# Block products for two more experts in the last batch, joined score bursts, a backlog rule and more H buffers in an attention and expert-mixture kernel

## The chip, the cores and the metric

The kernel runs on one core of one Trainium2 chip. The metric is the device time of one execution in microseconds. Times are medians of several executions. The record calls an execution slow when it takes over 1.5% more than the fastest one of the same kernel.

A profile shows one execution. Its span is about 1.7 us shorter than the time of that execution, some 0.5 to 2.7 us shorter than the median of the kernel, and its first 35 us vary by up to about 2 us from execution to execution, with the moment at which the first loads arrive. For differences of one or two microseconds I therefore also use the part of each trace that begins with a fixed instruction, a score burst at about 35 us, up to which all kernels here have the same TensorE instructions (298 records in a trace, or 299 where one more 512-column record was kept).

## The reference

```python
def _attn_ref(q, k, v, n_sink, window):          # (4, 8, 768, 64), n_sink 4, window 128
    scores = q @ k.T / sqrt(D)
    keep = (pos_k < n_sink) | ((rel >= 0) & (rel < window))
    a = softmax(where(keep, scores, -1e9))
    return a @ v

def _moe_ref(x, domain_probs, w1, w2):           # x (3072, 512), 4 experts, F 1024
    p = domain_probs / (domain_probs.sum(-1, keepdims=True) + 1e-9)
    for e in range(4):
        h = np.maximum(x @ w1[e], 0.0)
        out += p[:, e:e+1] * (h @ w2[e])
```

The attention output, with its heads side by side, is the input `x` of the mixture. Every token goes through all four experts.

## The kernel before

A scheduler written in Python orders the instructions when the kernel is built. It keeps a planned clock for each engine, and at each step it picks the next piece of TensorE work. The four batches go through in turn; while the mixture of one batch runs, the attention of the next batch is mixed in. From batch 1 on, tokens come in groups of 256 (three groups a batch).

A *first-layer unit* is one expert's `relu(x @ w1)` for one group. A plain unit takes 32 matmuls of 256 columns. A *fast* unit is a scheme of seven block products (P1 to P7) where a plain one has eight: 56 matmuls of 128 columns, with sums of weights and of tokens formed by VectorE, and with more VectorE and ScalarE work on the results. `START` says from which batch an expert is fast. The second layer uses such a scheme for every expert from batch 1 on; these are *the products* below (112 matmuls of 256 columns for a group).

```python
START = {0: 1, 1: 2}
CHAIN = ("P1", "P2", "P6", "P5", "P7", "P4", "P3")
NH = 6                                    # H buffers (outputs of first-layer units)

def emit_fast(self, u, m, ready):         # cut: one block product of a fast unit
    name = {"P1": "X", "P5": "V", "P6": "X", "P2": "Y", "P7": "X", "P3": "V", "P4": "X"}[m]
    ...
    if m == "P1":   ...   # ScalarE seeds tile Y with a copy of P1
    elif m == "P5": ...   # ScalarE keeps P5
    # both():  VectorE tensor_add(V, c5, X); only then may P7 and P3 start
    elif m == "P7": ...   # VectorE tensor_add(c5, c5, y); only then may P4 start
    # four results: VectorE max(.,0) * gate

def emit_product(self):                   # cut: second-layer products, two accumulators
    bank = int(m in ("P2", "P5", "P3"))
    ...
        if m == "P1": nc.scalar.copy(out=acc[1][:, 0:G], in_=x)
        if m == "P3": nc.vector.tensor_add(C12, C12, x)          # then store
        nc.scalar.copy(out={"P2": C11, "P6": C12, "P7": C22, "P4": C21}[m], in_=x)
        # P7: then VectorE adds P5 from acc[1] to C22

# the main loop: options are (ready, rank, kind, step); the lowest rank that is ready goes first
opts = [(max(r, now), 0 if due else 3, "att", step) for r, step in att.options()]
opts.append((max(p, now), 1 if mix.credit >= QF * G else 2.5, "product", None))
opts += [(max(f, now), 2, "first", x) for f, x in mix.firsts()]
```

Scores of two heads (one *burst*) use TensorE in halves of 64 rows, sink scores in quarters of 32 columns; everything else uses the whole array.

In this kernel a *bank* is a buffer that a group of matmuls writes. Another engine must copy or add its content out (the *evacuation*) before another group may use it. Names in the profile lines: `hps` is the bank of a plain unit, `cps` of a block product, `acc` of the second layer, `sps` of scores, `sinks` of sink scores, `od` of attention outputs. `H` is a unit's result, `T` a sum of tokens, `S` a sum of parts of `H`, `osb` the finished output, `qkT` the transposed rows.

The softmax here doesn't subtract the row's maximum and nothing guards it: scores larger than these inputs give would overflow.

Of the kernel before, what the change touches and what calls it, by code (L numbers as in the profile page):

```python
# [16 lines left out]
def kernel(  # L17
# [43 lines left out]
    START = {0: 1, 1: 2}  # L61
    ONACT = 1
    BIASED = 1
# [237 lines left out]
    def weight_form1(e):  # L301
# [3 lines left out]
        if e not in forms1:  # L305
            x = wpool.tile([P, 3, NDB // 2, F // 2], BF16, name=f"vf_{e}", tag=f"vf_{e}")
            forms1[e] = {"P1": A11, "P2": A12, "P3": x[:, 2], "P4": A22, "P5": x[:, 0], "P6": x[:, 1], "P7": A21}
            formed1[e] = 0
# [15 lines left out]
    def form1_due(e):  # L324
        n = formed1.get(e, 0)
        return landed.get(("w1", e), 1e12) < t["pe"] and (n < 3 or n == 3 and not left1[e])
# [233 lines left out]
    def sinks(b, piece):  # L560
# [3 lines left out]
        q0, q1 = piece * G, (piece + 1) * G  # L564
        ready = max([free_at(), keys_at[b]] + turned(b, piece))
# [10 lines left out]
        def run(engine):  # L576
# [5 lines left out]
            sinkA_at[b, piece] = at  # L582
        later("act", done, 800, run)

    def scores(b, hp, g):
        T = qkT[b]
        w = sum(x[2] for x in GROUPS[g]) * P
        ready = scores_ready(b, hp, g)
# [22 lines left out]
        scored_at[b] = done = pe(w, ready, n=6, switch=2)  # L611
# [32 lines left out]
    def scores_ready(b, hp, g):  # L644
        return max(free_at(2), *turned(b, g, hp))
# [98 lines left out]
    class Attention:  # L744


        def __init__(self, b):
# [3 lines left out]
            for g in range(NG):  # L751
# [3 lines left out]
                if g:  # L755
                    self.todo.insert(2 - NHP if b == 0 else -NHP, ("sinks", b, g, 0))
# [3 lines left out]
        def more(self):  # L760
            return bool(self.todo or self.scored or self.valued)

# [5 lines left out]
        def options(self):  # L768
# [5 lines left out]
            if self.todo:  # L774
                kind, b, x, y = self.todo[0]
                if kind == "scores":
                    if len(self.scored) < 4:
                        yield scores_ready(b, x, y), "todo"
                elif kind == "keys":
                    yield max(turned(b, 0)), "todo"  # L780
                elif kind == "sinks":
                    yield max([free_at(), keys_at.get(b, 1e12)] + turned(b, x)), "todo"
# [3 lines left out]
        def emit(self, step):  # L786
# [10 lines left out]
            elif step == "flip":  # L797
                _, b, g, hp = self.flips.pop(0)
                transposes(b, g, hp)
                if (b, g, hp) == (1, NG - 1, 0):  # L800
                    nat_loads(2, range(NQB))
                    turns.extend((2, tb) for tb in range(NQB))
            else:
# [4 lines left out]
                elif kind == "sinks":  # L808
                    sinks(b, x)
# [23 lines left out]
    CHAIN = ("P1", "P2", "P6", "P5", "P7", "P4", "P3")  # L833
# [3 lines left out]
    class Mixture:  # L837


        def __init__(self):  # L840
# [19 lines left out]
            self.stored = []  # L860

# [5 lines left out]

        def early_ready(self, g):
            if not self.early[g] or self.live >= NH:
# [5 lines left out]
        def opened(self, b, g, e):  # L875

            self.H[b, g, e] = mo.tile([P, 2, QF, 2, P], BF16, name="H", tag="H", bufs=NH)
            self.live += 1
# [12 lines left out]
        def begin(self):  # L891
# [3 lines left out]
            if self.units and self.live < NH:  # L895
                self.open.append(self.opened(*self.units.pop(0)))

        def widen(self):

            u = self.open[0]  # L900
            if len(self.open) == 1 and u["unit"][0] and len(u["left"]) < len(UNITS) and self.units and self.live < NH:
# [195 lines left out]
        def chore(self):  # L1097
# [12 lines left out]
            if self.last:  # L1110
                b, g, e = u = self.last[0]
                if (b, g, "P5") not in self.products:
# [56 lines left out]
        def emit_product(self):  # L1169
# [13 lines left out]
            self.piece = (k + 1) % E  # L1183
            if k < E - 1:
                return
            self.products.pop(0)
            if m == "P1":
                out_sb[b, g] = mo.tile([P, 2, Dout], FP32, name="osb", tag="osb", bufs=1)
                r = (b * NQB + 2 * g) * P
                self.C22[b, g] = join(2, lambda at: nc.sync.dma_start(out=out[r + P:r + 2 * P, :], in_=out_sb[b, g][:, 1]))  # L1190
            o = out_sb[b, g]
            C11, C12, C21, C22 = o[:, 0, 0:G], o[:, 0, G:], o[:, 1, 0:G], o[:, 1, G:]
            if m == "P5":
                acc_free[1] = end
                return
# [4 lines left out]
            def run(engine):  # L1200
                if m == "P1":
                    nc.scalar.copy(out=acc[1][:, 0:G], in_=x)  # L1202
                    acc_free[0] = acc_free[1] = act(G, seeded)
                    return
                if m == "P3":
# [4 lines left out]
                    return  # L1210
                nc.scalar.copy(out={"P2": C11, "P6": C12, "P7": C22, "P4": C21}[m], in_=x)  # L1211
                acc_free[bank] = at = act(G)
                if m == "P4":
                    sp(at)
                    self.C22[b, g](at)
                if m == "P7":
                    def add(engine):
                        nc.vector.tensor_add(C22, C22, acc[1][:, 0:G])
                        acc_free[1] = dve(G)
                        self.C22[b, g](acc_free[1])  # L1220
# [184 lines left out]
```

## Time and profile before

| | before |
|---|---|
| median of 4 runs | 379.08 us (378.89 to 379.22) |
| profiled span | 376.6 us |
| TensorE busy | 98% |
| VectorE busy | 72% |

The page of the kernel before gives the busy time of each engine, and the head of its chain of waits (shares of the span by engine):

```profile
PE 367.4 (98%) x3947; PEld 298.6 (79%) x3959; DVE 269.5 (72%) x610; ACT 148.4 (39%) x386; POOL 71.4 (19%) x91
...
PE 81%; DMA 13%; POOL 4%; issue 1%; DVE 0%; ACT 0%; POOLq 0%
```

The Trainium skill, "Perfetto Trace Analysis", section "Identifying the Most-Contended Engine", warns that the busy share of matmuls is a bad measure of distance from the limit, because pipelined instructions look smaller in the trace. So 98% alone proves nothing. Two other views do. The table of waits shows what TensorE waited for (engine, result and line, releaser: us in total, times, longest):

```profile
PE acc L484 <- DVE lent L398: 1.4, 1, 1.4
PE sps L604 <- DVE qkT L222: 1.1, 1, 1.1
...
PE acc L1178 <- ACT osb L1211: 0.5, 1, 0.5
PE acc L1178 <- ACT acc L1202: 0.4, 1, 0.4
```

The first two lie in the first 10 us, the last two in the final run of products; the three left out are a wait of 0.9 us for a weight load at 18 us and two of 0.2 us, at 36 and 72 us. And the timeline (start, length, instructions; the length includes the modelled end of the last matmul, so the pace is read from start to start) shows the pace:

```profile
33.53 1.89 PE L1248 MATMUL acc<-w,H 128*128 128x512 bf16 x8
35.35 0.62 PE L604 MATMUL sps<-qkT 64*128 64x128 bf16 x12
35.90 0.29 PE L569 MATMUL sinks<-qkT,ksd 128*32 128x256 bf16 x4
...
246.44 0.61 PE L1038 MATMUL cps<-T,w 128*128 128x128 bf16 x8
246.98 0.39 PE L604 MATMUL sps<-qkT 64*128 64x128 bf16 x6
247.31 1.05 PE L961 MATMUL hps<-xT,w 128*128 128x256 bf16 x8
...
264.73 1.91 PE L1178 MATMUL acc<-w,S 128*128 128x256 bf16 x16
266.48 1.91 PE L1178 MATMUL acc<-wf,H 128*128 128x256 bf16 x16
...
276.99 0.61 PE L1038 MATMUL cps<-xT,w 128*128 128x128 bf16 x8
277.43 0.61 PE L1038 MATMUL cps<-T,vf 128*128 128x128 bf16 x8
```

Sixteen matmuls of 256 columns take 1.75 us (109 ns each), eight of 128 columns 0.45 us (56 ns each): both stream at nearly the same pace per column. A score burst does not: the one at 246.98 us comes 0.09 us after the eight matmuls ahead of it are through (246.44 + 0.45), and the next instruction 0.33 us after its start.

For the last batch, windows give each engine's busy time in a stretch, with the number of instructions in brackets:

```profile
core 0: us, PE busy (x) PEld busy (x) DVE busy (x) ACT busy (x) POOL busy (x), PEclk, DMA share, GB/s
250.00:350.00 100.00, 100.00 (x1147) 92.25 (x1148) 76.12 (x162) 18.84 (x46) 0.00 (x0) 1.00 0.14 40
300.00:310.00 10.00, 10.00 (x125) 9.33 (x124) 9.69 (x19) 1.07 (x2) 0.00 (x0) 1.00 0.17 56
310.00:320.00 10.00, 10.00 (x107) 9.11 (x105) 7.04 (x19) 2.18 (x5) 0.00 (x0) 1.00 0.09 27
320.00:330.00 10.00, 10.00 (x113) 9.19 (x112) 7.44 (x16) 1.82 (x4) 0.00 (x0) 1.00 0.24 68
330.00:340.00 10.00, 10.00 (x129) 9.38 (x128) 9.79 (x20) 1.43 (x3) 0.00 (x0) 1.00 0.09 28
340.00:350.00 10.00, 10.00 (x103) 9.06 (x102) 3.86 (x9) 1.49 (x4) 0.00 (x0) 1.00 0.05 18
```

VectorE is 76% busy on the mean but uneven: nearly full while first-layer units run, lighter while products do. TensorE does not stop in these 100 us all the same.

### The profile page before, as it was taken

How to read it: one execution, taken by the hardware profiler on the slowest of the kernel's cores; microseconds unless marked ns; L12 is line 12 of the kernel's file. 1: busy time of each engine (PE TensorE's matmuls, PEld its weight loads, DVE VectorE, ACT ScalarE, POOL GpSimd, SP SyncE). 2: the span in 40 equal slices, each digit the busy share in tenths (PEclk: the TensorE clock that was granted, in tenths of full speed). 3: DMA queues.
4: the chain of work that ended last, by engine and by line, in shares of the span. 5: the costliest groups of instructions: out<-in, count | busy, mean ns of one | idle time of the engine just before them, and what ended most of it. 6: DMA issues, size and time to landing. Idle time of an engine off the chain costs nothing.

```text
span 376.6 us, 9443 instructions
## 1 busy us (share of the span) xinstructions
PE 367.4 (98%) x3947; PEld 298.6 (79%) x3959; DVE 269.5 (72%) x610; ACT 148.4 (39%) x386; POOL 71.4 (19%) x91
## 2 busy tenths in 40 slices
PE   7899999999999999999999999999999999999995
PEld 3585767667666788888888888889999999999984
DVE  5664988666345997696599499579499496795780
ACT  4854633675655144436315545362112011111110
POOL 8935114743322093010010000000000000000000
PEclk9999999999999999999999999999999999999999
DMA  9999999959697999148295211122011110200101
GB/s 167 167 185 202 210 210 174 152 40 178 60 125 150 179 145 146 67 47 58 66 153 136 52 63 30 30 82 61 28 58 30 57 31 29 71 30 2 57 1 57
DMA packets 110807, 35.61 MB, mean 95 GB/s; under 512 B 94260, under 2 KB 106132, under 8 KB 110764
## 3 DMA queue, kind: packets, MB, share of 16 engines
q0 software_dynamic: 77520, 17.31, 50.9%
q1 hardware_dynamic: 32188, 17.18, 20.7%
q10 hardware_dynamic: 1056, 0.52, 0.5%
q8 instruction: 31, 0.51, 0.5%
q14 instruction: 12, 0.10, 0.1%
HBM read 40.45 MB, written 6.34 MB: 124 GB/s over the span
## 4 chain that ended last, share of the span: by engine, by line
PE 81%; DMA 13%; POOL 4%; issue 1%; DVE 0%; ACT 0%; POOLq 0%
PE acc L1178 30%; PE hps L961 25%; PE cps L1038 13%; DMA w<-in_moe_w_dram 12%; PE acc L1248 6%; PE sps L604 3%; PE od L670 2%; DMA qkn<-in_q_dram 1%; POOL qkn L186 1%; PE tr L502 1%; POOL w L264 1%; POOL vx L251 1%; PE od L663 1%; POOL w L274 0%; POOL sel L417 0%
## 5 line engine op out<-in xcount | busy, mean ns | idle before, releaser
L961 PE MATMUL hps<-xT,w 128*128 128x256 bf16 x1056 | 131.6, 273 | 1.0 <-DMA w<-in_moe_w_dram 0.9
L961 PEld LDWEIGHTS <-w 128*128 128x128 bf16 x1056 | 99.1, 98 | 15.7 <-issue 1.9
L1178 PEld LDWEIGHTS <-H 128*128 128x128 bf16 x720 | 67.8, 98 | 10.5 <-issue 3.0
L629 ACT ACTIVATE aT<-sps 128x512 bf16<-128x512 f32 (+1 forms) x96 | 48.3, 568 | 38.1 <-PE sps L604 38.0
L985 DVE SCALAR_TENSOR_TENSOR H<-hps,gates 128x512 bf16<-128x512 f32 x84 | 56.9, 684 | 2.4 <-PE hps L961 1.3
L1178 PE MATMUL acc<-w,H 128*128 128x256 bf16 x432 | 56.4, 273 | 0.4 <-ACT acc L1202 0.4
L709 ACT ACTIVATE onat<-od,R 128x64 bf16<-128x64 f32 x144 | 33.0, 324 | 36.1 <-DVE R L697 36.0
L1248 PE MATMUL acc<-w,H 128*128 128x512 bf16 x180 | 43.6, 379 | 0.7 <-issue 0.2
L1211 ACT COPY osb<-acc 128x256 f32<-128x256 f32 x36 | 13.5, 374 | 57.4 <-PE acc L1178 54.2
L1178 PE MATMUL acc<-wf,H 128*128 128x256 bf16 x288 | 35.2, 273 | 0.5 <-ACT osb L1211 0.5
L251 POOL DMA_DIRECT2D vx<-in_v_dram x24 | 21.3, 898 | 72.0 <-PE od L670 63.0
L623 DVE TENSOR_TENSOR aT<-aT,mask 128x1024 bf16<-128x1024 bf16 (+1 forms) x36 | 22.9, 640 | 16.4 <-ACT aT L629 16.4
L1248 PEld LDWEIGHTS <-H 128*128 128x128 bf16 x192 | 18.1, 98 | 17.8 <-issue 0.3
L1038 PEld LDWEIGHTS <-w 128*128 128x128 bf16 x480 | 30.8, 98 | 1.8 <-issue 0.6
L1057 DVE SCALAR_TENSOR_TENSOR H<-cps,gates 128x512 bf16<-128x512 f32 x45 | 30.7, 684 | 0.2
L1178 PEld LDWEIGHTS <-S 128*128 128x128 bf16 x288 | 27.6, 98 | 3.8 <-issue 0.5
L974 ACT ACTIVATE H<-hps 128x512 bf16<-128x512 f32 x35 | 20.9, 598 | 24.2 <-PE hps L961 23.8
L1066 ACT COPY cps<-cps 128x512 f32<-128x512 f32 x15 | 8.7, 581 | 45.1 <-PE cps L1038 45.1
L1260 DVE SCALAR_TENSOR_TENSOR osb<-acc,scale_t,osb 128x512 f32<-128x512 f32 x18 | 13.5, 750 | 17.7 <-PE acc L1248 16.1
L186 POOL DMA_DIRECT2D qkn<-in_q_dram x22 | 19.9, 904 | 20.4 <-PE tr L502 12.2
L1038 PEld LDWEIGHTS <-vf 128*128 128x128 bf16 x360 | 22.6, 98 | 0.6
L186 POOL DMA_DIRECT2D qkn<-in_k_dram x22 | 20.0, 908 | 8.7 <-DMA w<-in_moe_w_dram 8.5
(96 smaller groups left out, 435.2 us busy)
## 6 DMA issues: line engine op xcount, KB each, us to landing
w<-in_moe_w_dram POOLq DMA_DIRECT2D x7, 1024.0 KB, 18.9
out_dram<-osb SPq DMA_DIRECT2D x24, 256.0 KB
gates<-gate_rows SPq DMA_DIRECT2D x36, 128.0 KB
vx<-in_v_dram POOLq DMA_DIRECT2D x24, 128.0 KB, 6.5
qkn<-in_q_dram POOLq DMA_DIRECT2D x22, 128.0 KB, 6.3
qkn<-in_k_dram POOLq DMA_DIRECT2D x22, 128.0 KB, 6.2
w<-in_moe_w_dram POOLq DMA_DIRECT2D x2, 512.0 KB, 9.3
kraw<-in_k_dram ACTq DMA_DIRECT2D x2, 256.0 KB
```

The source lines that it names most:

```text
L186: nc.gpsimd.dma_start(out=both[:, i], in_=src[b, :, tb * P:(tb + 1) * P, :].rearrange("h p d -> p h d"),)
L251: nc.gpsimd.dma_start(out=vx[tb][:, :, 0:D], in_=v[b, :, tb * P:(tb + 1) * P, :].rearrange("h p d -> p h d"),)
L623: nc.vector.tensor_mul(a, a, m[:, None, :].to_broadcast([P, 2, w]))
L629: nc.scalar.activation(out=a[:, ph], in_=sps[ph][:, 0:w], func=AF.Exp, scale=scale)
L709: nc.scalar.mul(o[:, qi, hp, ph * D:(ph + 1) * D], od[:, qi, ph, 0:D], R[:, qi, ph])
L961: nc.tensor.matmul(h[:, i].rearrange("p (q n) -> p q n", q=2), lhsT=w1_sb[e][:, db, fb * P:(fb + 1) * P], rhs=xT[b, g][:, :, db], start=(i ...
L974: nc.scalar.activation(out=dst, in_=h, func=AF.Relu)
L985: nc.vector.scalar_tensor_tensor(out=dst, in0=h, scalar=0.0, in1=gate, op0=ALU.max, op1=ALU.mult,)
L1038: nc.tensor.matmul(y[:, f], lhsT=A[:, d, f * P:(f + 1) * P], rhs=T[:, d], start=(m in ("P1", "P5") and f == 0 and d == 0), stop=(d == 1), ...
L1057: nc.vector.scalar_tensor_tensor(out=dst, in0=src, scalar=0.0, in1=gate, op0=ALU.max, op1=ALU.mult)
L1178: nc.tensor.matmul(x, lhsT=self.operand(b, g, e, m)[:, f], rhs=forms[e][m][:, f], start=(k == 0 and f == 0 and m in ("P1", "P5")), stop=(k ...
L1248: nc.tensor.matmul(op, lhsT=H[:, fb // QF, fb % QF, s], rhs=w2_sb[e][:, fb, :], start=(fb == 0), stop=(fb == NFB - 1),)
```

## The change

The intent: less TensorE work (block products for experts 2 and 3 in the last batch; fewer changes of TensorE's tiling), and a schedule that can bear VectorE's larger share (products go ahead when VectorE is behind; three more H buffers in the space of spent rows once attention ends; an output order in which products of one group alternate between the two accumulators).

```diff
-    START = {0: 1, 1: 2}
+    START = {0: 1, 1: 2, 2: 3, 3: 3}
+    ONE = 2
+    PAIR = 1
+    BEHIND = 800
@@ weight sums for experts that start in the last batch lie in spent q/k row tiles
+            if START[e] < B - 1: ...
+            else:
+                x = [sb.tile([P, 2, H, D], BF16, name="qkn", tag="qkn", bufs=NQB) for _ in range(3)]
@@ two score bursts in a row; one sink burst for two groups (b >= ONE)
+        def two(self):
+            return self.b >= PAIR and len(self.scored) <= 2 and len(self.todo) > 1 and ... == "scores"
+                    if self.two():
+                        yield scores_ready(b, x, y, 2), "two"
@@ H buffers in the space of the transposed rows, after attention
+        def room(self):
+            return self.spare or self.live < NH
+        def widened(self):
+            x = sb.tile([P, 2, NHP, S], BF16, name="qkT", tag="qkT", bufs=1)
+            self.spare = [ ... for i in range(3)]
@@ output order
-    CHAIN = ("P1", "P2", "P6", "P5", "P7", "P4", "P3")
+    CHAIN = ("P1", "P2", "P6", "P5", "P7", "P3", "P4")
+                elif m == "P7":
+                    nc.vector.tensor_add(C22, C22, x)
+                    acc_free[0] = at = dve(G)
+                else:
+                    nc.scalar.copy(out={"P2": C11, "P6": C12, "P5": C22, "P4": C21}[m], in_=x)
@@ when products go first
-        opts.append((max(p, now), 1 if mix.credit >= QF * G else 2.5, "product", None))
+        behind = max(t["dve"] - now, 0.0) + 500 * sum(x[2] == "dve" and x[0] < now + 300 for x in pend)
+        opts.append((max(p, now), 1 if behind > BEHIND else 2.5, "product", None))
... (cut: H buffers given back one by one, the last form of H due after P2, stores)
```

More of the change, by code (lines that the diff above doesn't have):

```diff
@@ L305, in weight_form1 @@
         if e not in forms1:
-            x = wpool.tile([P, 3, NDB // 2, F // 2], BF16, name=f"vf_{e}", tag=f"vf_{e}")
-            forms1[e] = {"P1": A11, "P2": A12, "P3": x[:, 2], "P4": A22, "P5": x[:, 0], "P6": x[:, 1], "P7": A21}
+            if START[e] < B - 1:
+                x = wpool.tile([P, 3, NDB // 2, F // 2], BF16, name=f"vf_{e}", tag=f"vf_{e}")
+                x = [x[:, i] for i in range(3)]
+            else:
+                x = [sb.tile([P, 2, H, D], BF16, name="qkn", tag="qkn", bufs=NQB) for _ in range(3)]
+                x = [i.rearrange("p d h c -> p d (h c)") for i in x]
+            forms1[e] = {"P1": A11, "P2": A12, "P3": x[2], "P4": A22, "P5": x[0], "P6": x[1], "P7": A21}
             formed1[e] = 0
@@ L325, in form1_due @@
         n = formed1.get(e, 0)
+        if START[e] == B - 1 and turned_at.get((B - 1, NQB - 1), 1e12) > t["pe"]:
+            return False
         return landed.get(("w1", e), 1e12) < t["pe"] and (n < 3 or n == 3 and not left1[e])
@@ L558, in turned, with sinks @@
         return [turned_at.get((b, tb), 1e12) for tb in range(2 * g + 2)]
-    def sinks(b, piece):
+    def sinks(b, piece, n=1):
         if b not in sinkA:
             sinkA[b] = sb.tile([P, 2 * G], BF16, name="sinkA", tag="sinkA", bufs=1)
-        q0, q1 = piece * G, (piece + 1) * G
-        ready = max([free_at(), keys_at[b]] + turned(b, piece))
+        q0, q1 = piece * G, (piece + n) * G
+        ready = sinks_ready(b, piece, n)
         slot = pick()
@@ L581, in run, with sinks_ready, scores @@
             take(slot, at)
-            sinkA_at[b, piece] = at
+            for i in range(n):
+                sinkA_at[b, piece + i] = at
         later("act", done, 800, run)
-    def scores(b, hp, g):
+    def sinks_ready(b, piece, n=1):
+        return max([free_at(), keys_at.get(b, 1e12)] + [x for i in range(n) for x in turned(b, piece + i)])
+    def scores(b, hp, g, more=False):
         T = qkT[b]
         w = sum(x[2] for x in GROUPS[g]) * P
-        ready = scores_ready(b, hp, g)
+        ready = 0.0 if more else scores_ready(b, hp, g)
         slots, sps = [], []
@@ L610, in scores @@
             c += nq * P
-        scored_at[b] = done = pe(w, ready, n=6, switch=2)
+        scored_at[b] = done = pe(w, ready, n=6, switch=0 if more else 2)
         a = sb.tile([P, 2, w], BF16, name="aT", tag="aT", bufs=4)
@@ L642, in scores, with scores_ready @@
         aTs[b, hp, g] = a
-    def scores_ready(b, hp, g):
-        return max(free_at(2), *turned(b, g, hp))
+    def scores_ready(b, hp, g, n=1):
+        return max([free_at(2 * n)] + [x for i in range(n) for x in turned(b, g, hp + i)])
     def values(b, hp, g):
@@ L754, in __init__ @@
                 self.todo += [("scores", b, hp, g) for hp in range(NHP)]
-                if g:
-                    self.todo.insert(2 - NHP if b == 0 else -NHP, ("sinks", b, g, 0))
+                if g and (b < ONE or g == 1):
+                    self.todo.insert(2 - NHP if b == 0 else -NHP, ("sinks", b, g, 1 if b < ONE else 2))
             self.total = len(self.todo) + len(self.flips) + (1 if b else 2) * NG * NHP
@@ L761, in more @@
             return bool(self.todo or self.scored or self.valued)
+        def two(self):
+            return self.b >= PAIR and len(self.scored) <= 2 and len(self.todo) > 1 and self.todo[0][::3] == self.todo[1][::3] and self.todo[0][0] == "scores"
         def flip_ready(self):
@@ L781, in options @@
                 elif kind == "sinks":
-                    yield max([free_at(), keys_at.get(b, 1e12)] + turned(b, x)), "todo"
+                    yield sinks_ready(b, x, y), "todo"
             if self.flips:
@@ L802, in emit @@
                     turns.extend((2, tb) for tb in range(NQB))
+            elif step == "two":
+                self.steps += 1
+                for i in range(2):
+                    _, b, x, y = self.todo.pop(0)
+                    scores(b, x, y, i)
+                    self.scored.append((b, x, y))
             else:
@@ L808, in emit @@
                 elif kind == "sinks":
-                    sinks(b, x)
+                    sinks(b, x, y)
                 elif kind == "keys":
@@ L860, in __init__ @@
             self.stored = []
+            self.spare, self.lent = [], {}
         def is_fast(self, b, e):
@@ L866, in more @@
             return bool(self.open or any(self.early.values()) or self.units or self.second or self.products)
+        def room(self):
+            return self.spare or self.live < NH
+        def widened(self):
+            x = sb.tile([P, 2, NHP, S], BF16, name="qkT", tag="qkT", bufs=1)
+            x = x.rearrange("p i h n -> p (i h n)")
+            n = 2 * QF * 2 * P
+            self.spare = [x[:, i * n:(i + 1) * n].rearrange("p (k f t n) -> p k f t n", k=2, f=QF, t=2) for i in range(3)]
         def early_ready(self, g):
-            if not self.early[g] or self.live >= NH:
+            if not self.early[g] or not self.room():
                 return 1e12
@@ L875, in opened @@
         def opened(self, b, g, e):
-            self.H[b, g, e] = mo.tile([P, 2, QF, 2, P], BF16, name="H", tag="H", bufs=NH)
-            self.live += 1
+            if self.spare:
+                self.H[b, g, e] = self.spare.pop()
+                self.lent[b, g, e] = self.H[b, g, e]
+            else:
+                self.H[b, g, e] = mo.tile([P, 2, QF, 2, P], BF16, name="H", tag="H", bufs=NH)
+                self.live += 1
             fast = self.is_fast(b, e)
@@ L894, in begin @@
                 return
-            if self.units and self.live < NH:
+            if self.units and self.room():
                 self.open.append(self.opened(*self.units.pop(0)))
@@ L900, in widen @@
             u = self.open[0]
-            if len(self.open) == 1 and u["unit"][0] and len(u["left"]) < len(UNITS) and self.units and self.live < NH:
+            if len(self.open) == 1 and u["unit"][0] and len(u["left"]) < len(UNITS) and self.units and self.room():
                 b, g, e = self.units[0]
@@ L1111, in chore @@
                 b, g, e = u = self.last[0]
-                if (b, g, "P5") not in self.products:
+                if (b, g, "P2") not in self.products:
                     self.last.pop(0)
@@ L1183, in emit_product @@
             self.piece = (k + 1) % E
+            if m == CHAIN[-1]:
+                if (b, g, e) in self.lent:
+                    self.spare.append(self.lent.pop((b, g, e)))
+                else:
+                    self.live -= 1
             if k < E - 1:
@@ L1189, in emit_product, with store @@
                 r = (b * NQB + 2 * g) * P
-                self.C22[b, g] = join(2, lambda at: nc.sync.dma_start(out=out[r + P:r + 2 * P, :], in_=out_sb[b, g][:, 1]))
+                def store(at):
+                    nc.sync.dma_start(out=out[r + P:r + 2 * P, :], in_=out_sb[b, g][:, 1])
+                    sp(at)
+                self.C22[b, g] = join(2, store)
             o = out_sb[b, g]
             C11, C12, C21, C22 = o[:, 0, 0:G], o[:, 0, G:], o[:, 1, 0:G], o[:, 1, G:]
-            if m == "P5":
-                acc_free[1] = end
-                return
             acc_free[bank], seeded = 1e12, acc_free[1]
@@ L1203, in run @@
                     acc_free[0] = acc_free[1] = act(G, seeded)
-                    return
-                if m == "P3":
+                elif m == "P3":
                     nc.vector.tensor_add(C12, C12, x)
@@ L1209, in run @@
                     sp(at)
-                    return
-                nc.scalar.copy(out={"P2": C11, "P6": C12, "P7": C22, "P4": C21}[m], in_=x)
-                acc_free[bank] = at = act(G)
-                if m == "P4":
-                    sp(at)
-                    self.C22[b, g](at)
-                if m == "P7":
-                    def add(engine):
-                        nc.vector.tensor_add(C22, C22, acc[1][:, 0:G])
-                        acc_free[1] = dve(G)
-                        self.C22[b, g](acc_free[1])
-                    acc_free[1] = 1e12
-                    later("dve", at, 300, add)
+                elif m == "P7":
+                    nc.vector.tensor_add(C22, C22, x)
+                    acc_free[0] = at = dve(G)
+                    self.C22[b, g](at)
+                else:
+                    nc.scalar.copy(out={"P2": C11, "P6": C12, "P5": C22, "P4": C21}[m], in_=x)
+                    acc_free[bank] = at = act(G)
+                    if m == "P4":
+                        self.C22[b, g](at)
             r = (b * NQB + 2 * g) * P
-            later("dve" if m == "P3" else "act", end, 200, run)
-            if m == "P3":
-                self.live -= E
+            later("dve" if m in ("P3", "P7") else "act", end, 200, run)
         def second_ready(self):
@@ L1282 @@
     work = [E * NG * 2 * NFB * NDB * G] + [NG * E * NFB * G * (NDB + 7 / 4) - NG * sum(mix.is_fast(b, e) for e in FAST) * NFB * P for b in range(1, B)]
-    ahead, upto, loaded = 0, 0.0, 0
+    ahead, upto, loaded, wide = 0, 0.0, 0, 0
     loads, turns = [(load_nat, 0, tb) for tb in (4, 5)] + [(load_v, 0, (4, 5))], []
@@ L1307 @@
         now = t["pe"]
+        if not att.more() and ahead == B - 1 and not wide:
+            wide = 1
+            mix.widened()
         if not att.more() and not loaded:
@@ L1340 @@
         if att.more():
-            opts = [(max(r, now), 0 if due else 3, "att", step) for r, step in att.options()]
+            opts = [(max(r, now), (0 if due else 3) - 0.1 * (step == "two"), "att", step) for r, step in att.options()]
         s2, p = mix.second_ready(), mix.product_ready()
-        opts.append((max(p, now), 1 if mix.credit >= QF * G else 2.5, "product", None))
+        behind = max(t["dve"] - now, 0.0) + 500 * sum(x[2] == "dve" and x[0] < now + 300 for x in pend)
+        opts.append((max(p, now), 1 if behind > BEHIND else 2.5, "product", None))
         opts += [(max(f, now), 2, "first", x) for f, x in mix.firsts()]
```

## The prediction

> **What bounds the kernel now.** TensorE. The page gives PE 367.4 of 376.6 us (98%); the table of waits gives PE seven waits, 4.7 us in all, and after 130 us only two, 0.45 and 0.46 us, both in the final run of products. The chain of waits is 81% PE. In the timeline 16 matmuls of 256 columns take 1.745 us (109 ns each), 8 of 128 columns 0.447 us (56 ns each), so narrow matmuls lose nothing. The granted clock is 1.0. The time follows the sum of PE's work; I cost the change as that sum, from both kernels' instruction lists.
>
> **What it removes, adds and moves.**
>
> 1. Block products for experts 2 and 3 in the last batch: six units change from 32 matmuls of 256 columns (3.49 us) to 56 of 128 (3.13 us): 192 wide matmuls go (-20.9 us), 336 narrow come (+18.8), plus one 512-column matmul that marks a bank (+0.2). Net -2.0 us.
> 2. Joined score bursts: a lone burst of six 128-column matmuls starts about 0.1 us late and the next instruction comes 0.33 us after: 0.43 us for 0.23 us of streaming. A burst of twelve, already there at 35 us, took 0.09 + 0.55 us. Each join saves about 0.2 us. The Trainium skill, "TensorEngine Tiling (Array Packing)", Key Properties, says a change of tiling mode drains TensorE; this 0.2 us per burst agrees. The order has 31 contiguous runs of unbiased score matmuls instead of 44: -2.6 us.
> 3. Sink bursts: eight become six, -0.4 us.
> 4. New output order: the wait of P4 for the copy of P7 (0.46 us in the last group) goes. But P4 and the next group's P1 now share a bank, and the new kernel ends with 168 product matmuls in a row, which hold that boundary: about 0.46 us returns there; the wait between P1 and P2 (0.45 us) stays. Net 0. The 3.4 us tail stays.
> 5. Nine H buffers, borrowed space and the product rule by VectorE's backlog remove no PE work. As PE shows almost no gaps, they only keep step 1 from stalling.
>
> **Load on VectorE.** A fast unit has six 512-column fp32 operations (0.60 us apart back to back), a slow one four. A last-batch group goes from about 19 to 21.5 us of VectorE per 24.7 us of PE: under 90%. Forming the weights adds eight operations, 4.9 us, around the end of attention, where VectorE is already 98% busy for 10 us. I allow 0.4 us of new PE waits. ScalarE has ample room.
>
> **Critical path.** All this PE work lies on it: -2.0 - 2.6 - 0.4 = -5.0 us, +0.4 for waits. The first 80 us are the same instructions.
>
> **Prediction: 374.5 us**, 8 times in 10 between 373.0 and 376.3. Faster by over 2%: 0.05; within 2%: 0.93; slower by over 2%: 0.02.
>
> **What would show it.** Block matmuls 1176 instead of 840 at the same 56 ns (step 1). Twelve-matmul score bursts costing about 0.64 us (step 2). In the last 20 us two PE waits of about 0.45 us, at P4/P1 and before P2 (step 4). VectorE's sum up by about 13 us, PE's total waits up by under 1 us (step 5).
>
> **What would make it wrong.** If PE waits on VectorE chains in the all-block last batch, the gain shrinks: 376 or more. If joined bursts wait for exponentials or banks, step 2 shrinks. If PE has hidden gaps between 20 and 250 us that the backlog rule closes, the gain could reach 7 us.

## The result, and the profile after

| | before | after |
|---|---|---|
| median | 379.08 us (4 runs) | 374.60 us (4 runs, 373.97 to 375.52) |
| ratio of fast runs | | 0.9884, 95% interval 0.9862 to 0.9906 |
| profiled span | 376.6 us | 373.0 us |
| TensorE busy | 98% | 97% |
| VectorE busy | 72% | 76% |

A ratio is the mean time of one kernel's fast runs over that of the other's of the same rounds, so it is not quite the ratio of the medians. The change is an improvement of 1.2%. Five more rounds, told below, gave 375.33 us and 0.9902. TensorE has 137 instructions more in the trace: 336 narrow matmuls and the bank-marking one came, 192 wide ones and eight sink matmuls went, as the change intends.

The page of the kernel after:

```profile
PE 363.2 (97%) x4084; PEld 300.8 (81%) x4096; DVE 284.6 (76%) x630; ACT 153.1 (41%) x396; POOL 71.5 (19%) x91
```

Its table of waits for TensorE:

```profile
PE acc L1218 <- ACT osb L1259: 1.0, 2, 0.5
...
PE acc L1218 <- ACT acc L1247: 0.4, 1, 0.4
PE hps L1001 <- DVE H L1016: 0.4, 1, 0.4
```

Two of these are new: one more wait for `osb` (a finished product's copy, at 204 us), and one for a first-layer evacuation (`H`, at 94 us). The timeline shows both, a joined burst of twelve (its follower comes 0.55 us after its start, as at 35 us in the kernel before), and the two waits in the last run of products:

```profile
94.22 1.03 PE L1001 MATMUL hps<-xT,w 128*128 128x256 bf16 x8 [0.41 <-DVE H L1016]
...
105.22 0.62 PE L618 MATMUL sps<-qkT 64*128 64x128 bf16 x12
105.77 1.05 PE L1001 MATMUL hps<-xT,w 128*128 128x256 bf16 x8
...
204.57 1.03 PE L1218 MATMUL acc<-w,S 128*128 128x256 bf16 x8 [0.54 <-ACT osb L1259]
...
356.63 1.91 PE L1218 MATMUL acc<-w,H 128*128 128x256 bf16 x16 [0.46 <-ACT osb L1259]
358.99 1.91 PE L1218 MATMUL acc<-w,H 128*128 128x256 bf16 x16 [0.45 <-ACT acc L1247]
```

Windows of the last batch, with the columns as before:

```profile
250.00:350.00 100.00, 100.00 (x1325) 94.22 (x1323) 90.30 (x181) 24.32 (x55) 0.00 (x0) 1.00 0.13 40
300.00:310.00 10.00, 10.00 (x127) 9.26 (x126) 9.83 (x25) 2.12 (x5) 0.00 (x0) 1.00 0.21 64
310.00:320.00 10.00, 10.00 (x148) 9.59 (x146) 9.07 (x16) 2.74 (x6) 0.00 (x0) 1.00 0.11 36
320.00:330.00 10.00, 10.00 (x125) 9.31 (x123) 8.53 (x19) 1.82 (x4) 0.00 (x0) 1.00 0.05 16
330.00:340.00 10.00, 10.00 (x159) 9.72 (x157) 9.35 (x19) 3.53 (x8) 0.00 (x0) 1.00 0.15 54
```

VectorE's share of the last batch rose from 76 to 90%, and it is now even: no 10 us stretch from 250 to 350 us is below 83%. TensorE still does not stop.

### Where the time went: an account of TensorE

I split the time from the start of the fixed burst at 35 us to the start of the last matmul into three parts, from the start of every TensorE matmul in the trace.

- *Streaming*: each matmul's columns at the pace read above (0.417 ns a column plus 2.4 ns, which gives 109 and 56 ns); score matmuls are counted as running two at a time and sink matmuls four at a time, so theirs are divided by two and four. This is a convention; it does not touch the differences, as every trace has the same 216 score matmuls from 35 us on. Where the trace lacks records of 512-column matmuls, their streaming is added; eleven lack in the traces of before and after.
- *Switching*: what the instructions at the borders of, and inside, score and sink bursts take beyond that. It holds any wait that falls there.
- *Rest*: all that is left, which is waits and small gaps.

| us | whole | streaming | switching | rest |
|---|---|---|---|---|
| before | 337.6 | 325.0 | 9.5 | 3.1 |
| after, first trace | 334.0 | 323.0 | 6.4 | 4.6 |
| after, second trace (run `again`) | 334.5 | 323.0 | 6.4 | 5.1 |

Streaming fell by 2.0 us, as predicted for the block products. Switching fell by 3.1 us, as predicted for the bursts (3.0). But the rest grew by 1.5 to 2.0 us where 0.4 had been allowed. The two new waits are 1.3 us of it in the first trace and 1.5 us in the second, from start to start (the brackets count from the modelled end of the last matmul and show some 0.16 us less for each); the remainder lies in gaps too small for the table of waits and is not explained.

### The profile page after: what moved, and what is told of

Its sections match the earlier page's. It is cut to its first block, busy times and chain, and to the rows that moved or that the text cites. A ratio compares the mean times of both kernels' runs of the same rounds, so it can differ in the third digit from the quotient of the medians.

```text
span 373.0 us, 9781 instructions
## 1 busy us (share of the span) xinstructions
PE 363.2 (97%) x4084; PEld 300.8 (81%) x4096; DVE 284.6 (76%) x630; ACT 153.1 (41%) x396; POOL 71.5 (19%) x91
## 4 chain that ended last, share of the span: by engine, by line
PE 75%; DMA 15%; POOL 3%; ACT 3%; DVE 2%; issue 1%; POOLq 0%; ACTq 0%; DVEq 0%
PE acc L1218 29%; PE hps L1001 18%; PE cps L1078 17%; DMA w<-in_moe_w_dram 13%; PE acc L1286 5%; PE sps L618 2%; PE od L684 2%; DMA xT<-onat 2%; POOL qkn L189 1%; ACT onat L723 1%; DMA qkn<-in_q_dram 1%; PE tr L512 1%; POOL w L267 1%; ACT aT L643 1%; PE od L677 1%
## 5 line engine op out<-in xcount | busy, mean ns | idle before, releaser
L1001 PE MATMUL hps<-xT,w 128*128 128x256 bf16 x864 | 107.0, 273 | 1.3 <-DMA w<-in_moe_w_dram 0.9
L1001 PEld LDWEIGHTS <-w 128*128 128x128 bf16 x864 | 82.0, 98 | 14.4 <-issue 2.0
L1218 PEld LDWEIGHTS <-H 128*128 128x128 bf16 x600 | 56.0, 98 | 7.6 <-issue 1.9
L643 ACT ACTIVATE aT<-sps 128x512 bf16<-128x512 f32 (+1 forms) x96 | 47.0, 574 | 31.3 <-PE sps L618 31.2
L723 ACT ACTIVATE onat<-od,R 128x64 bf16<-128x64 f32 x144 | 33.3, 331 | 39.7 <-DVE R L711 39.7
L1218 PE MATMUL acc<-w,H 128*128 128x256 bf16 x360 | 47.7, 273 | 1.0 <-ACT osb L1259 0.5
L1025 DVE SCALAR_TENSOR_TENSOR H<-hps,gates 128x512 bf16<-128x512 f32 x56 | 38.0, 686 | 12.4 <-PE hps L1001 12.2
L1078 PEld LDWEIGHTS <-w 128*128 128x128 bf16 x672 | 42.4, 98 | 1.9 <-issue 0.5
L1259 ACT COPY osb<-acc 128x256 f32<-128x256 f32 x36 | 13.6, 384 | 52.8 <-PE acc L1218 51.9
L1097 DVE SCALAR_TENSOR_TENSOR H<-cps,gates 128x512 bf16<-128x512 f32 x48 | 32.8, 685 | 2.1 <-PE cps L1078 1.3
L1286 PEld LDWEIGHTS <-H 128*128 128x128 bf16 x192 | 18.3, 98 | 17.5
L1218 PE MATMUL acc<-wf,H 128*128 128x256 bf16 x240 | 31.9, 273 | 0.0
L1106 ACT COPY cps<-cps 128x512 f32<-128x512 f32 x21 | 12.1, 576 | 42.2 <-PE cps L1078 40.6
L1078 PE MATMUL cps<-T,w 128*128 128x128 bf16 x336 | 25.6, 219 | 0.0
L1078 PE MATMUL cps<-xT,w 128*128 128x128 bf16 x336 | 25.3, 219 | 0.0
```

The costliest lines, as they stand in the source:

```text
L643: nc.scalar.activation(out=a[:, ph], in_=sps[ph][:, 0:w], func=AF.Exp, scale=scale)
L723: nc.scalar.mul(o[:, qi, hp, ph * D:(ph + 1) * D], od[:, qi, ph, 0:D], R[:, qi, ph])
L1001: nc.tensor.matmul(h[:, i].rearrange("p (q n) -> p q n", q=2), lhsT=w1_sb[e][:, db, fb * P:(fb + 1) * P], rhs=xT[b, g][:, :, db], start=(i ...
L1025: nc.vector.scalar_tensor_tensor(out=dst, in0=h, scalar=0.0, in1=gate, op0=ALU.max, op1=ALU.mult,)
L1078: nc.tensor.matmul(y[:, f], lhsT=A[:, d, f * P:(f + 1) * P], rhs=T[:, d], start=(m in ("P1", "P5") and f == 0 and d == 0), stop=(d == 1), ...
L1097: nc.vector.scalar_tensor_tensor(out=dst, in0=src, scalar=0.0, in1=gate, op0=ALU.max, op1=ALU.mult)
```

## The experiments

The theory: the time is the sum of TensorE's work, so each part of the change is worth what it takes off that sum, and the rule and the buffers only keep the block units from stalling. The rival: part of these sums is lost in new waits or, the other way, the schedule is worth time of its own. Every run used 5 rounds. All outputs are right. Times are medians; the ratio is to the kernel before in the same rounds (that kernel's median was 378.67 to 379.19 us in the three sets of runs, 11 runs each). Where the trace's account matters, it is given as streaming / switching / rest.

### again: the changed kernel once more

No edit.

> The changed kernel once more, unchanged, so that its time rests on more rounds. 374.6 us, ratio to the kernel before 0.988, between 0.986 and 0.990. Every theory expects this; a ratio over 0.991 would say that the first four runs were lucky.

Measured: 375.33 us, ratio 0.9902 (0.9884 to 0.9921), just outside the 0.986 to 0.990 that were expected, and short of the 0.991 that would have called the first runs lucky. Taking both sets, the gain is 1.0 to 1.2%.

### no_blocks: the block products undone

```diff
-    START = {0: 1, 1: 2, 2: 3, 3: 3}
+    START = {0: 1, 1: 2}
```

> The changed kernel with plain first-layer products for experts 2 and 3 in the last batch, everything else kept. Theory (the time is the sum of TensorE's work): 192 wide matmuls come back for 336 narrow ones and the bank-marking matmul, +2.0 us, 376.6 us; no new waits of TensorE, and VectorE's busy sum falls by about 13 us to some 271 us. Rival (with VectorE 90% busy in the last batch the block units make TensorE wait, so the saved columns are lost there): 374.3 to 375.2 us, and TensorE's last matmul ends less than 0.8 us later than in the changed kernel.

Measured: 376.93 us, ratio 0.9947 (0.9930 to 0.9964), against 0.9902 for `again` in the same rounds: 1.7 us slower. The account is 325.0 / 6.3 / 5.2: streaming is back by exactly 2.0 us and the rest is the same. VectorE's sum fell from 284.9 to 274.2 us, by 10.7 us and not 13. The rival fell: its 374.3 to 375.2 us did not come. But "no new waits" was wrong: the wait at 204 us is gone, and three others come (0.5 us at 94, 0.2 at 231, 0.4 at 349 us by the table of waits). That the rest is the same on both sides is a sum of different waits.

### no_joins: single bursts

```diff
-    ONE = 2
-    PAIR = 1
+    ONE = 4
+    PAIR = 4
```

> The changed kernel with single score bursts and single sink bursts, everything else kept. Theory (each joined burst saves one tiling-mode switch of about 0.2 us on TensorE): 13 score bursts and 2 sink bursts more, +3.0 us, 377.6 us. Rival (the joined bursts hand ScalarE four exponentials at once and hold four banks; the one wait of 0.54 us for ScalarE at 204 us in the changed kernel is the visible part, and it eats the gain): +1.5 us or less, 376.1 us or less.

Measured: 376.26 us, ratio 0.9926 (0.9910 to 0.9941): 0.9 us slower than `again`. Here the rival held, by the difference (its 376.1 us was counted from 374.6 us). The account is 322.8 / 9.5 / 2.9 against 323.0 / 6.4 / 5.1 of `again`: the joins save 3.1 us of switching, and they bring 2.2 us of waits and small gaps. With single bursts both the wait for `H` at 94 us and the one for `osb` at 204 us are absent from the table of waits.

The other traces tell the two apart. The wait at 94 us stands in all traces with joined bursts in which the token sums are not delayed, and in none of the three without joins (`before`, `no_joins`, `blocks_alone`). The wait at 204 us is absent also from `no_blocks`, `credit` and `old_order`, which have the joins: it needs the joins and this order of work together.

### tail: two more banks for the last group

The last run of products has nothing to fill its waits with. By then the first layer's six banks are idle, so this kernel lends two of them to the last group and orders that group P1 P5 P6 P2 P7 P3 P4.

```diff
+    TAIL = ("P1", "P5", "P6", "P2", "P7", "P3", "P4")
+        def bank_of(self, b, g, m):
+            if (b, g) == PAIRS[-1]:
+                return 1 if m == "P2" else 3 if m in ("P5", "P3") else 2
+            return int(m in ("P2", "P5", "P3"))
... (cut: taking two tiles of the ring at the last P1, and bank_of in place of the old rule)
```

> The changed kernel with two more accumulator banks for the last group alone, lent by the first layer, which is over by then, in the order P1 P5 P6 P2 P7 P3 P4, so that no product follows another into a bank that must first be copied out. Theory (the two waits of 0.46 and 0.45 us in the last run of products lie on the critical path): both waits gone, -0.9 us, 373.7 us. Rival (the end is set by the last evacuation and store, or the waits only move to the forms of H): 374.4 us or more.

Measured: 373.98 us, ratio 0.9876 (0.9856 to 0.9896), 1.0 us below `again` by the ratios. Both waits of the last run are gone from the table of waits, and the rest fell from 5.1 to 4.0 us. The two waits were on the critical path. This agrees with the Trainium skill, "Perfetto Trace Analysis", "Optimizing Tensor Performance", Matmuls, which advises that independent groups rotate through banks so that the evacuation of one overlaps the matmuls of the next.

### six_H: without the three lent H buffers

```diff
-    ahead, upto, loaded, wide = 0, 0.0, 0, 0
+    ahead, upto, loaded, wide = 0, 0.0, 0, 1
```

> The changed kernel with six H buffers to the end: the row space is never lent. Theory (more H buffers remove no TensorE work and only keep the block units from stalling): between 0 and +2.0 us against the changed kernel run twice before (374.6 and 375.3 us), that is up to 377 us; if it costs anything, the new TensorE waits lie between 250 and 350 us. Rival (nine buffers do nothing, VectorE below 90% in a group leaves enough room with six): less than 0.3 us either way and no new wait after 250 us.

Measured: 376.36 us, ratio 0.9939 (0.9922 to 0.9955), about 1.4 us above `again` by the ratios (other rounds). The account is 323.0 / 6.1 / 6.6. The new waits are at 311, 336 and 359 us, all inside block units, for VectorE's results; the last, the longest with 0.8 us, lies outside the stretch that the theory had named. The buffers are worth something, as the theory had it.

### credit: with the old rule for products

```diff
-        opts.append((max(p, now), 1 if behind > BEHIND else 2.5, "product", None))
+        opts.append((max(p, now), 1 if mix.credit >= QF * G else 2.5, "product", None))
```

> The changed kernel with the old rule for when products go first (a credit of first-layer columns) in place of VectorE's backlog. Theory (the rule removes no work; under the old rule TensorE waits on VectorE in the all-block last batch, where it needs products between block units): +0.5 to +2.0 us over the changed kernel, with new TensorE waits after 250 us. Rival (the rule is idle decoration here): within 0.3 us and the same waits.

Measured: 380.76 us, ratio 1.0057 (1.0042 to 1.0072): 5.9 us above `again` by the ratios, and slower than the kernel before. The direction was right, but the size was three times the most that had been expected. The table of waits gains 3.0 us in five waits of `cps` (block products) for VectorE's sum `both`. Switching rose as well, from 6.4 to 8.1 us: two bursts fewer are joined, and two waits of 0.6 us in all fall ahead of bursts, at 213 us.

### six_H_credit: neither help

Both edits above together.

> Both schedule helps taken away: six H buffers to the end and the old credit rule, with block products and joined bursts kept. Theory: the block products' gain of 2.0 us is partly lost to waits in the last batch, 375.5 to 377 us. Rival: both helps are worth nothing, 374.5 to 375.5 us.

Measured: 390.17 us, ratio 1.0309 (1.0287 to 1.0330): about 15 us above `again`, and 3% above the kernel before. Nothing of the kind was expected. The account is 323.2 / 8.1 / 17.8. Its windows of the last batch, to be held against those of before and after:

```profile
250.00:350.00 100.00, 92.23 (x1159) 84.60 (x1157) 77.66 (x165) 23.26 (x52) 0.00 (x0) 0.98 0.14 40
300.00:310.00 10.00, 10.00 (x118) 9.24 (x116) 4.05 (x10) 2.10 (x6) 0.00 (x0) 1.00 0.17 61
310.00:320.00 10.00, 9.21 (x140) 8.73 (x138) 9.47 (x18) 2.96 (x6) 0.00 (x0) 1.00 0.13 28
320.00:330.00 10.00, 7.16 (x88) 6.08 (x87) 8.49 (x20) 1.33 (x3) 0.00 (x0) 0.92 0.09 26
330.00:340.00 10.00, 10.00 (x101) 8.79 (x100) 3.22 (x9) 1.82 (x4) 0.00 (x0) 0.91 0.16 57
```

VectorE swings between a third busy and full, as it does in the kernel before (39% at 340 us, 98% at 330 us), where TensorE does not stop: the unevenness alone is not the cause. The granted clock dipped to 0.92 and 0.91 in two of these stretches; over the whole execution it was 0.996; 0.4% of 389 us is 1.6 us, an estimate, and too little to explain 15 us. The timeline shows how TensorE stops:

```profile
296.26 0.61 PE L1078 MATMUL cps<-T,w 128*128 128x128 bf16 x8 [0.73 <-DVE H L1128]
299.07 0.61 PE L1218 MATMUL acc<-wf,S 128*128 128x256 bf16 x4 [2.20 <-DVE S L1178]
```

A block unit waits for a sum on VectorE. Next in TensorE's order are products, and these wait for the sums of H (`S`), which stand in VectorE's queue behind the block units' own operations (L1097):

```profile
297.06 1.28 DVE L1097 SCALAR_TENSOR_TENSOR H<-cps,gates 128x512 bf16<-128x512 f32 x2
298.26 0.41 DVE L1178 TENSOR_TENSOR H<-H 128x512 bf16<-128x512 bf16 x1
298.60 0.41 DVE L1178 TENSOR_TENSOR S<-S,H 128x512 bf16<-128x512 bf16 x1
```

Then come 10 us of products in which VectorE has little to do.

### blocks_alone: the block products in the kernel before

```diff
-    START = {0: 1, 1: 2}
+    START = {0: 1, 1: 2, 2: 3, 3: 3}
... (cut: the weight sums in spent row tiles and their start, as in the change)
```

> The kernel before with the block products for experts 2 and 3 in the last batch alone (space borrowed as in the changed kernel); old rule, old order, single bursts, six H buffers. Theory (sum of TensorE's work, no new waits): -2.0 us, 377.1 us against 379.1. If the old schedule makes TensorE wait in the all-block batch: 377.8 to 379.5 us, with waits in the trace after 250 us.

Measured: 382.48 us, ratio 1.0096 (1.0080 to 1.0113): 3.6 us *slower* than the kernel before, beyond the range of either theory. The account is 322.8 / 9.5 / 9.6: streaming is 2.2 us less than in the kernel before, switching is the same, and the rest grew by 6.5 us. The largest new entry in its table of waits:

```profile
PE cps L1045 <- DVE cps L1080: 3.3, 5, 0.8
```

### joins_only: joined bursts and new order, without blocks and without helps

The edits of `no_blocks`, `six_H` and `credit` together.

> The changed kernel without the block products of experts 2 and 3, with the old credit rule and six H buffers to the end: what is left is the joined bursts and the new output order. It has the schedule that cost 15 us with the block products. Theory (rule and buffers matter only because the last batch is all block units, near VectorE's limit): without those units the old schedule costs nothing, so the time is within 0.7 us of the run without blocks but with both helps (376.9 us), and no TensorE wait for VectorE after 250 us. Rival (the helps are worth several us by themselves, whatever the units): 379 us or more.

Measured: 376.97 us, ratio 0.9950 (0.9930 to 0.9970), against 376.93 us and 0.9947 for `no_blocks`, which has the rule and the buffers. So without block products for experts 2 and 3 the helps are worth nothing on balance, and with them 15 us. On balance only: the account is 325.4 / 7.1 / 3.5 against 325.0 / 6.3 / 5.2, so with the helps switching is 0.8 us less and the rest 1.7 us more. No wait for VectorE after 250 us appears in the table of waits.

### old_order: P4 before P3 again

```diff
-    CHAIN = ("P1", "P2", "P6", "P5", "P7", "P3", "P4")
+    CHAIN = ("P1", "P2", "P6", "P5", "P7", "P4", "P3")
```

> The changed kernel with P4 before P3 again, everything else kept. Theory (the order only moves the conflict over a bank from P7/P4 inside a group to P4/P1 between groups, and the last run of products holds one such place either way): within 0.5 us of the changed kernel (374.6 and 375.3 us), with one TensorE wait of about 0.5 us moved from the boundary to P4 of the last group. Rival (the order is worth something of its own): 376 us or more.

Measured: 376.33 us, ratio 0.9943 (0.9921 to 0.9966), some 1.0 to 1.6 us slower than `again` (other rounds; the two intervals just touch). The rest is 6.6 us. TensorE now waits three times, 2.1 us in all, for VectorE's addition of P7, twice outside the last group too. The order is worth something, so the theory's zero was wrong. One caution: the changed kernel takes P7 out by VectorE, which is busy in the last batch, and this run keeps that. The old order with the old evacuation by ScalarE was not run. Nor were the smaller edits of the change alone (H buffers given back one by one, the last form of H due after P2).

### tail_late and tail_late_any: the two waits that came with the joins

At 91 us VectorE of the changed kernel stands idle, in front of a token sum (`T`) whose input a DMA has not yet brought; the work queued behind it comes late, down to the first-layer evacuation at 93.49 us (L1016) that TensorE waits for at 94.22 us. From VectorE's timeline of the kernel after:

```profile
91.29 0.29 DVE L1052 TENSOR_TENSOR T<-xT 128x256 bf16<-128x256 bf16 x1 [1.96 <-DMA xT<-onat]
91.62 0.29 DVE L1052 TENSOR_TENSOR T<-xT,T 128x256 bf16<-128x256 bf16 x1
91.83 0.68 DVE L1016 TENSOR_SCALAR H<-hps 128x512 bf16<-128x512 f32 x1
...
93.49 0.68 DVE L1016 TENSOR_SCALAR H<-hps 128x512 bf16<-128x512 f32 x1
```

At 204 us the copy of P2 (L1259) stands on ScalarE behind the exponentials (L643, L587) and the multiplications (L723). From ScalarE's timeline of the kernel after:

```profile
201.78 1.17 ACT L643 ACTIVATE aT<-sps 128x512 bf16<-128x512 f32 x2
202.73 0.71 ACT L587 ACTIVATE sinkA<-sinks 128x512 bf16<-128x512 f32 x1
203.21 1.05 ACT L723 ACTIVATE onat<-od,R 128x64 bf16<-128x64 f32 x4
203.99 0.80 ACT L1259 COPY osb<-acc 128x256 f32<-128x256 f32 x2
```

Both runs build on `tail`. `tail_late`:

```diff
-            if at > t["pe"]:
+            if at > t["pe"] - WAITED:        # WAITED = 2000 ns
```

> The kernel with two more banks for the last group, and with the token sums of the block products queued on VectorE 2 us later than its plan says their transposed input lands. In the trace of the changed kernel VectorE stands 1.96 us at such a sum for a DMA at 91 us, a first-layer evacuation queues behind it, and TensorE then waits 0.41 us. Theory: that wait goes, 0.4 to 0.8 us better than the kernel with the banks alone (374.0 us): 373.2 to 373.6 us. Rival (the wait is due to the joined bursts' banks): no change.

Measured: 372.54 us, ratio 0.9840 (0.9819 to 0.9860), against 0.9876 for `tail` (other rounds): 1.4 us better, more than expected; in the trace the rest fell from 4.0 to 3.1 us. The wait at 94 us is gone from the table of waits. The edit delays every token sum, not this one alone, so not all of the 1.4 us need come from this wait.

`tail_late_any`:

```diff
-                    nc.scalar.copy(out={"P2": C11, ...}[m], in_=x)
-                    acc_free[home] = at = act(G)
+                    copy(engine, {"P2": C11, ...}[m], x)
+                    acc_free[home] = at = clock(engine, G)
-            later("dve" if m in ("P3", "P7") else "act", end, 200, run)
+            later("dve" if m in ("P3", "P7") else "act" if m == "P1" else "any", end, 200, run)
```

> As the run before, and the copies of finished products go to ScalarE or VectorE, whichever is free first (4 of 36 go to VectorE). At 204 us in the changed kernel TensorE waits 0.54 us for the copy of P2, which stands on ScalarE behind the exponentials of joined bursts. Theory: that wait goes as well, another 0.4 to 0.7 us: 372.6 to 373.1 us, the fastest kernel here. Rival (the copies on VectorE delay others): no gain or a loss.

Measured: 372.40 us, ratio 0.9830 (0.9812 to 0.9848). The copy of P2 is now done by VectorE at 202.13 us, the wait at 204 us is gone, and the rest is 2.3 us, below that of the kernel before; but 0.1 us between the medians is not told apart by the times. The account, 323.0 / 6.4 / 2.3, has all the joins' and the blocks' savings and none of these waits; one of 0.3 us is new, at 172 us. This kernel beats both: 1.7% under the kernel before.

### The account of all runs

| us | time (median) | ratio | streaming | switching | rest |
|---|---|---|---|---|---|
| before | 378.67 to 379.19 | 1 | 325.0 | 9.5 | 3.1 |
| again (the change) | 375.33 | 0.9902 | 323.0 | 6.4 | 5.1 |
| no_blocks | 376.93 | 0.9947 | 325.0 | 6.3 | 5.2 |
| no_joins | 376.26 | 0.9926 | 322.8 | 9.5 | 2.9 |
| joins_only | 376.97 | 0.9950 | 325.4 | 7.1 | 3.5 |
| blocks_alone | 382.48 | 1.0096 | 322.8 | 9.5 | 9.6 |
| six_H | 376.36 | 0.9939 | 323.0 | 6.1 | 6.6 |
| credit | 380.76 | 1.0057 | 323.2 | 8.1 | 9.1 |
| six_H_credit | 390.17 | 1.0309 | 323.2 | 8.1 | 17.8 |
| old_order | 376.33 | 0.9943 | 323.0 | 6.2 | 6.6 |
| tail | 373.98 | 0.9876 | 323.0 | 6.4 | 4.0 |
| tail_late | 372.54 | 0.9840 | 323.0 | 6.2 | 3.1 |
| tail_late_any | 372.40 | 0.9830 | 323.0 | 6.4 | 2.3 |

## Why the prediction was right, and which terms were mis-sized

The predicted time was 374.5 us; measured were 374.60 and, in more rounds, 375.33 us. The mechanism (TensorE's sum decides) held, and the term for new waits was too small. That the first median lies within 0.1 us is partly luck: the traces show a gain of 3.0 to 3.5 us after 35 us and not 4.6.

- **What bounds the kernel.** Right for the changed kernel. Where streaming alone changed on balance (`no_blocks`, 2.0 us), the time followed (1.7 us). Where waits changed as well (`no_joins`, `blocks_alone`), the time was the sum of both, not that of TensorE's work.
- **Step 1, block products: -2.0 us.** Right: streaming fell by 2.0 us, and undoing them cost 1.7 us by the ratios. It holds only with the rest of the change: in the kernel before, the same products cost 3.6 us.
- **Steps 2 and 3, joined bursts: -3.0 us of switching.** The switching itself was right, 3.1 us. The term that failed is the allowance "I allow 0.4 us of new PE waits", which the prediction tied to VectorE at the end of attention. Measured were 1.5 to 2.0 us of waits and small gaps, of which the two waits at 94 and 204 us are 1.3 to 1.5 us: `no_joins` has neither. The prediction came near this under what would make it wrong ("If joined bursts wait for exponentials or banks, step 2 shrinks"), but it is not the bursts that wait: other work waits behind theirs. As they stand, the joins are worth 0.9 us and not 3.0. That VectorE's queue and ScalarE's queue are the causes is shown for both: with each queue mended, its wait went. The second wait is not due to the joins alone, as said above.
- **Step 4, output order: net 0.** The two waits stood where the prediction put them, at the border P4/P1 (0.46 us) and ahead of P2 (0.45 us). Between the two kernels the net is zero, as predicted: the kernel before has two waits of the same length. What the prediction did not see is that the order is needed once P7 is evacuated by VectorE: the old order then costs 1.0 to 1.6 us, with waits outside the last group too.
- **Step 5, buffers and rule.** "They only keep step 1 from stalling" was right, and shown: without block products they are worth nothing on balance (376.97 against 376.93 us). What I did not foresee, in the expectations either, is the size: 15 us with both taken away, and far more than the sum of the two singly (1.4 and 5.9 us).
- **Load on VectorE.** 21.5 us for 24.7 us of TensorE is 87%; measured were 90%. Its sum rose by 15 us (13 predicted). The argument "under 90%, so few waits" was too weak: from 250 to 350 us `six_H_credit` has VectorE 78% busy and loses most of its 15 us from there on, while the changed kernel has it 90% busy and TensorE does not stop. Nor does the evenness decide: in the kernel before VectorE is as uneven, and TensorE does not stop. What the timeline of `six_H_credit` shows is that the next work in TensorE's order, a block unit and then products, waited for VectorE's queue. The mean does not show that; the waits do.

The predicted sum, -5.0 + 0.4 = -4.6 us, compares with -3.0 to -3.5 us in the traces after 35 us and with -3.7 to -4.5 us in the times. Most of the difference between these two comes from the executions that were traced: that of the kernel before took 378.30 us, 0.8 us less than the median, and those of the change took 374.73 and 375.54 us, so between traced executions the gain is 3.6 and 2.8 us. What makes executions of one kernel differ by that much, no run settles.

## What to carry to other kernels

When the bounding engine has almost no gaps, cost a change as the sum of its work, and then look separately for what the change puts into the other engines' queues: here the joined bursts changed the order on ScalarE and VectorE just where an evacuation was due. A change that shifts work to a second engine needs, as I read these traces, an order that gives the first one other work while the second is behind; the same block products gave -1.7 us in the one schedule and +3.6 us in the other. The Trainium skill, "Perfetto Trace Analysis", section "Optimization Strategy", says that regimes with different limits may be interleaved to gain time; this agrees, with 15 us between a last batch that mixes products and block units by VectorE's backlog, with nine buffers, and one that does not.

## What the Trainium skill lacked or had wrong

- "TensorEngine Tiling (Array Packing)", Key Properties: a change of tiling mode drains TensorE, as the page says, but it gives no cost. Here 36 score bursts after 35 us had 7.9 us of switching and 23 had 5.5 us: about 0.2 us for each burst that was saved.
- "Perfetto Trace Analysis", Identifying the Most-Contended Engine: the page offers occupancy as the measure for VectorE. Here VectorE is the second engine, and its occupancy did not tell whether TensorE stops: from 250 to 350 us, 78% went with a TensorE that stopped for 8% of the stretch, 76% and 90% with one that never did. The table of waits told it.
- "Perfetto Trace Analysis", Optimizing Tensor Performance, Matmuls: larger matmuls are called more efficient when possible. Here the gap is small: two matmuls of 128 columns take 112 ns and one of 256 takes 109 ns, and trading 192 of the larger for 336 of the smaller, with an eighth fewer columns in all, was a gain of 2 us.
